# Last modulation row's outer product scaled on VectorE, the other three rows two scalings per piece on ScalarE and stored from its own queue; one more matmul piece ahead of the last norm gradient

## The chip, the cores and the metric

The kernel runs on one core of a Trainium2 chip. The metric is the device time of one execution in microseconds (us), and the number that stands for a kernel is the median of its runs. One further execution is recorded by the hardware profiler; it has a time of its own. Five engines run their own instruction streams in order: TensorE (PE), VectorE (DVE), ScalarE (ACT), GpSimd (POOL) and SyncE (SP). SP, ACT and POOL also issue DMAs from their queues.

## The reference

The kernel computes the forward pass and all gradients of a conditioned block: six modulation rows come from a condition vector, a layer norm is scaled and shifted by them and goes through a spectral mixer (FFT, a learned complex weight, inverse FFT), and a second norm goes through a two-layer MLP.

```python
mod = (silu(c) @ w_mod).reshape(c.shape[0], 6, 1, -1)      # six rows sa, ca, ga, sb, cb, gb of 1024
h = layernorm(x) * (1 + ca) + sa
x = x + ga * irfft2(rfft2(h) * (w_r + 1j * w_i))           # x is 2048 x 1024
h = layernorm(x) * (1 + cb) + sb
x = x + gb * (gelu(layernorm(h) @ w1 + b1) @ w2 + b2)      # w1 is 1024 x 3584
# outputs: x, and the gradients of x, w_r, w_i, w1, b1, w2, b2, c and w_mod (1024 x 6144)
```

Two of the gradients matter here. The gradient of `w1` (1024 x 3584, `out_4`) is a product over 2048 tokens. The gradient of `w_mod` (`out_9`) is an outer product: column block r of it, 1024 x 1024, is `u = silu(c)` times the gradient `gmod[r]` of modulation row r. The same row also goes, multiplied by `w_mod` and summed, into the gradient of `c`.

## The kernel before, in words

The last stretch of the program, some 90 us, is the gradient of `w1`. A generator, `pieces`, cuts it into pieces of matrix products; `fill(n)` writes out the next n of them. A plain piece is one 128 x 512 block: 16 matmuls over the 16 token chunks into a PSUM accumulator `gw1acc` (four of them rotate under one tag), a cast by ACT into a ring of eight `gwo` buffers, and a store by POOL. Feature groups 0 to 4 are done so. Groups 5 and 6 go together (`gw1_quads`) by seven products in place of eight: a piece there is two products of 8 matmuls each, ACT copies an accumulator into `snap`, DVE adds accumulators and snaps into `gwo`, and some accumulators are cast straight into `gwo`. The second product into an accumulator `gqy` may only start when ACT has copied the first out into `snap`. Its operands (`ct`, `gzh`) are sums that DVE makes beforehand in `quad_sums`. The PE writes out its pieces in one fixed order.

Other work is written out between the pieces, and each engine runs its own share in order:

- `consume_bwd(i, ...)` is the last of the backward mixer, called for four chunks of tokens. Chunk 3 makes the last norm gradient. DVE reduces rows into `s1c` (`scaled_rows`) and `sc` (`ln_bwd`), ACT scales (L1368), `fill` puts plain pieces between. At its end the column sum `accCA` is halved (ACT copy, DVE sum into `rows`) and stored to DRAM as `gmod[1]` by two DMAs of SP (L229).
- After it, `gmod[0]` is made: ACT copies `accSA` into `sr`, DVE folds `sr` and casts it to `row` (L200), and SP stores that row (L201).
- `gmod_chain` goes over rows 4, 2, 1, 0 and eight 128 x 1024 blocks of `w_mod` for each: SP loads the row, broadcast to 128 partitions, into `gr` (L1279, one buffer per row) and the blocks into a ring of four `wrw` (L1280, four steps ahead), and DVE multiplies and sums (L1287). Ten of its 32 steps are written ahead of the loop below.
- `gmod_scaled` goes over the same rows and makes `out_9`: 32 scalings of `gr` by a column of `u_rt` into a ring of five buffers `otl`, each then stored (256 KB).

The loop that closes the program takes the last 23 pieces, n = 0 to 22: the first eight are the plain pieces of group 4, the others fifteen of the sixteen quad pieces. Behind each piece it writes out chain steps (from n = 7 on) and scalings: one for n below 14, two from 14 on. The last piece follows the loop, beside the gradient of `c` (`gc_bf`, a product `ptr`).

DMAs issued by SP and by ACT count their landing on eight counters, DMAHW0 to DMAHW7, dealt out in turn in the order of the program. In the rows below, what a DMA "waits" on can therefore be data, or the previous DMA with the same counter, which must have landed first. DMAs of POOL have counters of their own (DMASW).

Of the kernel before, what the change touches and what calls it, by code (L numbers as in the profile page):

```python
# [13 lines left out]
ACT = mybir.ActivationFunctionType  # L14
ALU = mybir.AluOpType
AX = mybir.AxisListType

P = 128
S = 2048
D = 1024  # L20
# [15 lines left out]
def kernel(  # L36
# [24 lines left out]
    nc = tc.nc  # L61
# [11 lines left out]
    def ps_s(name):  # L73
        return psum.tile([P, 512], FP32, tag="s", name=name)
# [51 lines left out]
    def chunk_rows(dt, i):  # L126
        return dt[4 * i * P:4 * (i + 1) * P, :].rearrange("(q p) d -> p q d", p=P)
# [14 lines left out]
    def load_tok(t4, src, i, eng=None):  # L142
        s3 = tok_flat(src)
        ins = (eng or nc.sync).dma_start(out=tok_plain(t4, i), in_=tok_rows(s3, i, 0, D))
        for q in range(2):
            nc.gpsimd.indirect_dma_start(out=t4[:, tok_idx(i, q), :], out_offset=None, in_=s3,
                                         in_offset=bass.IndirectOffsetOnAxis(ap=xidx[:, 2 * i + q:2 * i + q + 1], axis=0))
        return ins
# [45 lines left out]
    def tt(out, a, b, op):  # L194
        return nc.vector.tensor_tensor(out=out, in0=a, in1=b, op=op)  # L195
# [125 lines left out]
    def unfold_d(o4, tmp):  # L321
        n = o4.shape[1]
        ov = o4.rearrange("p c (a b w) -> p c a b w", b=2, w=256)
        tv = tmp.rearrange("p c (s b w) -> p c s b w", s=2, w=256)
        tt(tv[:, :, 0], ov[:, :, :, 0, :], ov[:, :, :, 1, :], ALU.add)
        tt(tv[:, :, 1], ov[:, :, :, 0, :], ov[:, :, :, 1, :], ALU.subtract)
        fwd = o4.rearrange("p c (b w) -> p c b w", w=512)[:, :, :, 0:256]
        rev = bass.AP(tensor=o4.tensor, offset=o4.offset + 1023, ap=[o4.ap[0], [D, n], [-512, 2], [-1, 256]])
        tt(fwd, tv[:, :, :, 0, :], tv[:, :, :, 1, :], ALU.add)
        tt(rev, tv[:, :, :, 0, :], tv[:, :, :, 1, :], ALU.subtract)  # L330

    def unfold_tok(o4, tmp):
        tt(tmp[:, 0:4:2, :], o4[:, 0:4:2, :], o4[:, 1:4:2, :], ALU.add)
        tt(tmp[:, 1:4:2, :], o4[:, 0:4:2, :], o4[:, 1:4:2, :], ALU.subtract)
        tt(o4[:, 0:4:3, :], tmp[:, 0:2, :], tmp[:, 2:4, :], ALU.add)
        tt(o4[:, 1:3, :], tmp[:, 0:2, :], tmp[:, 2:4, :], ALU.subtract)
# [84 lines left out]
    for cl, colv, modn in ((CE, kev, 2048), (SE, kev, 2048), (CO, kod, 4096), (SO, kod, 4096)):  # L421
        rows, n = (rowo, 4) if cl % 2 else (rowe, 2)
# [87 lines left out]
    def norm_act(out4, in4, row, i, qs=range(4)):  # L510
        norm_in[0] = ()
        for q in qs:
            t = 4 * i + q
            norm_in[0] += (nc.scalar.activation(out=out4[:, q, :], in_=in4[:, q, :], func=ACT.Identity,  # L514
                                                scale=stats[:, row, 0, t:t + 1], bias=stats[:, row, 1, t:t + 1]),)
# [17 lines left out]
    def ph_out(fc, j, pp):  # L533
        ph2 = phs[fc % 4]
        q = (0, 2, 3, 1)[j]
        ov = ph2[:, :, q * P:(q + 1) * P]
        pv = pp[:, :].rearrange("p (i w) -> p i w", w=P)
        copy = nc.any.tensor_copy if fc <= PH_EARLY else nc.vector.tensor_copy if fc >= PH_KEEP and j > 1 else nc.scalar.copy
        with tc.high_priority():
            copy(out=ov, in_=pv)  # L540
        if j == 3:
            nc.gpsimd.dma_start(out=d_ph[fc * P:(fc + 1) * P, :], in_=ph2.rearrange("p i w -> p (i w)"))

    def ph_part(fc, js):
        for j in js:
# [3 lines left out]
                                              start=(cch == 0), stop=(cch == NDC - 1))  # L549
            ph_out(fc, j, pp)  # L550

    turn_in = [None, None]

    def turn_go(j, cch):
# [20 lines left out]
    for j in range(4):  # L575
        n = 0
# [33 lines left out]
    def gen_rows():  # L610
# [5 lines left out]
        nc.gpsimd.tensor_scalar(out=em1[:, 1, 4:6, 255:256], in0=em1[:, 0, 4:6, 255:256], scalar1=1.0 / (S * D), scalar2=None, op0=ALU.mult)  # L616
        nc.gpsimd.dma_start(out=d_E[:], in_=em1[:])
        return em1

    def behind(ins, later):  # L620
        tc.add_manual_dep(ins.ins, later.ins.name, mybir.DependencyInfo(mybir.DependencyClass.NoSync, mybir.DependencyReason.DATA),
                          reason="order")

    last_pu = [None]
    last_po = [None]
# [19 lines left out]
    w1g = {}  # L645
# [606 lines left out]
    u_rt = small.tile([P, NDC], FP32, tag="u_rt", bufs=1)  # L1252
# [40 lines left out]
    def gmod_scaled(rows):  # L1293
        for n in range(len(rows) * NDC):
            k, jc = n // NDC, n % NDC
            gw, r = w1g["gw"][n % 5], rows[k]
            with tc.issue_after(w1g["ev"].ins):
                nc.scalar.activation(out=gw, in_=w1g["gr"][k], func=ACT.Identity, scale=u_rt[:, jc:jc + 1])
            nc.gpsimd.dma_start(out=out_9[jc * P:(jc + 1) * P, r * D:(r + 1) * D], in_=gw)
            yield  # L1300

    step_in = []
# [276 lines left out]
    accCA = []  # L1579

    chain, scaled = gmod_chain((4, 2, 1, 0)), gmod_scaled((4, 2, 1, 0))
    prods = []

    def consume_bwd(i, o4, tmp, tmp2, n1, eb):
        if i == 0:
            accCA.append(ps_s("accCA"))
            nc.vector.tensor_copy(out=sacc, in_=eb[:, 0, :])
        elif i == 2:
            tt(sacc, sacc, eb[:, 0, :], ALU.add)
        if i == 3:  # L1590
            x1_in = nc.sync.dma_start(out=eb, in_=chunk_rows(d_gx1, i))
        unfold_d(o4, tmp)
        unfold_tok(o4, tmp)
        load_tok(n1, A_x, i, nc.gpsimd)
        with tc.issue_after(last_po[0].ins):
            norm_act(n1, n1, 0, i)
        prods.append(tt(tmp, o4, n1, ALU.mult))
        fill((0, 6, 6, 8)[i])
        s1c = small.tile([P, 4], FP32, tag="s1c")
        scaled_rows(o4, o4, opca_row, s1c, 0, i)  # L1600
        for q in range(4):
            ln_bwd(o4[:, q, :], s1c[:, q:q + 1], n1[:, q, :], tmp2[:, q, :],
                   (lambda: tc.issue_after(w1g["ev"].ins)) if i else ExitStack)
        if i < 3:
            x1_in = nc.sync.dma_start(out=n1, in_=chunk_rows(d_gx1, i))
        tt(o4, o4, n1 if i < 3 else eb, ALU.add)
        store_tok(out_1, o4, i)
        if i == 1:
            with tc.issue_after(x1_in.ins):
                next(chain)  # L1610
        fill((4, 1, 2, 2)[i])
        halves_sum(accCA[0], tmp, i == 0, i == 3)
        fill((1, 2, 1, 2)[i])
        if i == 3:
            rows = small.tile([P, D], BF16, tag="gmrow", bufs=1)
            store_halves(accCA[0], rows[0:64, 0:KH], tmp, 1)
# [165 lines left out]
    def fill(n):  # L1782
        for _ in range(n):
            next(todo)
        done[0] += n
# [28 lines left out]
    with tc.issue_after(fm_in.ins):  # L1814
        for jc in range(NDC):
            wr = wr5[jc // 4][:, jc % 4, :]
            nc.vector.tensor_tensor_reduce(out=wr, in0=wr, in1=gr5[:], scale=1.0, scalar=0.0,
                                           op0=ALU.mult, op1=ALU.add, accum_out=gu[:, 5, jc:jc + 1])
# [39 lines left out]
    left = NFC * 4 - 1 - done[0]  # L1858
    for n in range(left):
        fill(1)  # L1860
        k = [(32 - CHAIN_EARLY) * min(max(n + 17 + j - left, 0), 14) // 14 for j in range(2)]
        for _ in range(k[1] - k[0]):
            with tc.issue_after(w1g["dve"].ins):
                next(chain)
        for _ in range(2 if n >= left - 9 else 1):
            next(scaled, None)
    fin2 = reg.tile([P, 2, P], BF16, name="fin2", tag="ph")
    make_identity(nc, fin2[:, 0, :])
# [41 lines left out]
```

## Time and profile before

| what | value |
|---|---|
| median of 3 runs | 1373.33 us (1371.58, 1376.87, 1373.33) |
| the profiled execution, its own time | 1372.29 us |
| its span in the profile | 1370.3 us |
| mean granted clock of TensorE | 0.997 |
| ACT scalings `otl<-gr,u_rt` | 32, from 1291.3 us to 1361.3 us |
| last ACT cast into `gwo` begins | 1363.14 us |
| DVE, ACT, POOL busy | 79%, 58%, 28% of the span |

The span is the profiler's, from the first to the last instruction that it records; the execution's time is 2.0 us longer. All positions in time below are counted from the start of the span. In the timeline a row is a start, a length, the engine, the source line, what it does, a count, and in brackets how long the engine sat idle before it and what released it. SPq and ACTq are the issuing of DMAs by those engines.

### The profile page before, as it was taken

What the parts mean: (1) busy time and instruction counts of PE and PEld (TensorE: products, weight loads), DVE (VectorE), ACT (ScalarE), POOL (GpSimd) and SP (SyncE); (2) the same over time, 40 slices, a digit from 0 to 9 for tenths busy, and PEclk for the clock granted to TensorE, in tenths of its full rate; (3) what the DMA queues carried; (4) which work ended last, traced back from release to release, by engine and by line L of the source; (5) the groups of instructions that cost most, each with busy time, mean ns of one, the idle gap of its engine ahead of it and who ended that gap; (6) DMA issues with size and microseconds to landing.
All of it is one profiled execution on the core that took longest, in us unless ns stands there. A gap on an engine that the chain in (4) does not pass through costs nothing. (4 is left out here: it accounts for less than half of the span.)

```text
span 1370.3 us, 18631 instructions
## 1 busy us (share of the span) xinstructions
PE 1345.6 (98%) x6899; PEld 651.0 (48%) x6899; DVE 1077.2 (79%) x1467; ACT 792.4 (58%) x1120; POOL 390.3 (28%) x436
## 2 busy tenths in 40 slices
PE   7999999999999999999999999999999999999997
PEld 4445566444444444444444444444644555444443
DVE  6997889999988878787620578889888488976985
ACT  4864667767877765665414593445732554544456
POOL 6273642411112122212211010112344330332163
PEclk9999999999999999999999999999999999999999
DMA  9975594899787887698999699988579878899876
GB/s 326 322 196 140 160 256 154 250 279 318 262 254 252 212 261 246 199 289 233 284 278 224 181 217 311 296 254 257 179 238 270 222 160 237 207 245 251 201 271 244
DMA packets 356401, 330.08 MB, mean 241 GB/s; under 512 B 203866, under 2 KB 298736, under 8 KB 356182
## 3 DMA queue, kind: packets, MB, share of 16 engines
q1 hardware_dynamic: 314310, 201.02, 57.2%
q0 software_dynamic: 35232, 120.00, 26.0%
q10 hardware_dynamic: 6768, 7.87, 1.7%
q8 instruction: 54, 0.88, 0.3%
q14 instruction: 37, 0.30, 0.1%
HBM read 165.73 MB, written 114.87 MB: 205 GB/s over the span
## 5 line engine op out<-in xcount | busy, mean ns | idle before, releaser
L1230 PE MATMUL pg<-w1T,gzr 128*128 128x512 bf16 x896 | 195.8, 380 | 0.0
L548 PE MATMUL pp<-gBoT,wt 128*128 128x512 bf16 x832 | 185.4, 379 | 3.2 <-ACT pho L540 1.9
L1076 PEld LDWEIGHTS <-w 128*128 128x128 bf16 x896 | 87.2, 98 | 107.4 <-issue 2.9
L1230 PEld LDWEIGHTS <-gzr 128*128 128x128 bf16 x896 | 86.5, 98 | 108.5 <-issue 5.8
L548 PEld LDWEIGHTS <-wt 128*128 128x128 bf16 x832 | 81.0, 98 | 97.9 <-issue 5.3
L1770 PE MATMUL gw1acc<-gzh,n3n 128*128 128x512 bf16 x512 | 111.8, 380 | 0.0
L1076 PE MATMUL pz<-n3Ta,w 128*128 128x512 bf16 x448 | 98.8, 380 | 1.4 <-ACT gt L1079 1.4
L1076 PE MATMUL pz<-n3Tb,w 128*128 128x512 bf16 x448 | 99.0, 380 | 0.0
L1770 PEld LDWEIGHTS <-n3n 128*128 128x128 bf16 x640 | 62.3, 98 | 76.7 <-issue 3.1
L195 DVE TENSOR_TENSOR ct<-ct 128x2048 bf16<-128x2048 bf16 (+1 forms) x84 | 91.5, 1120 | 4.3 <-ACT n L514 2.0
L1079 ACT ACTIVATE gt<-pz,b_col 128x512 bf16<-128x512 f32 x112 | 72.8, 682 | 37.3 <-PE pz L1076 33.1
L1130 PEld LDWEIGHTS <-hhA 128*128 128x128 bf16 x608 | 58.9, 98 | 73.2 <-issue 3.0
L1087 ACT ACTIVATE gt<-gt 128x2048 bf16<-128x2048 bf16 x28 | 53.5, 1911 | 58.3 <-DVE gt L195 58.3
L1411 PE MATMUL gw2acc<-gB,hhsA 128*128 128x512 bf16 x384 | 84.8, 380 | 0.0
L195 DVE TENSOR_TENSOR gt<-gt,gt 128x2048 bf16<-128x2048 bf16 x56 | 68.4, 1223 | 17.7 <-ACT gt L1089 16.8
L1419 ACT CAST gwo<-gw2acc 128x512 bf16<-128x512 f32 x40 | 23.5, 588 | 87.5 <-PE gw2acc L1411 84.2
L1411 PEld LDWEIGHTS <-hhsA 128*128 128x128 bf16 x384 | 37.5, 98 | 43.5
L1083 ACT ACTIVATE gt<-gt 128x2048 bf16<-128x2048 bf16 x28 | 53.4, 1908 | 3.1 <-DVE hhC L195 2.4
L540 ACT CAST pho<-pp 128x512 bf16<-128x512 f32 x68 | 38.6, 584 | 27.3 <-PE pp L548 24.1
L1774 ACT CAST gwo<-gw1acc 128x512 bf16<-128x512 f32 x40 | 23.0, 579 | 53.6 <-PE gw1acc L1770 41.6
L1089 ACT ACTIVATE gt<-gt 128x2048 bf16<-128x2048 bf16 x28 | 53.3, 1905 | 0.3
L1411 PE MATMUL gw2acc<-gB,otl 128*128 128x512 bf16 x224 | 50.0, 380 | 0.0
(414 smaller groups left out, 2710.3 us busy)
## 6 DMA issues: line engine op xcount, KB each, us to landing
gzr<-d_gz SPq DMA_DIRECT2D x28, 512.0 KB
d_ph<-pho POOLq DMA_DIRECT2D x21, 512.0 KB, 5.5
wblk<-in_w_mod_dram SPq DMA_DIRECT2D x10, 1024.0 KB
out_dram<-otl POOLq DMA_DIRECT2D x40, 256.0 KB, 4.1
d_hh<-hhA POOLq DMA_DIRECT2D x19, 512.0 KB, 5.6
wrw<-in_w_mod_dram SPq DMA_DIRECT2D x32, 256.0 KB
w<-in_B_w_dram SPq DMA_DIRECT2D x7, 1024.0 KB
hhC<-d_ph SPq DMA_DIRECT2D x14, 512.0 KB
```

The costliest lines, as they stand in the source:

```text
L195: return nc.vector.tensor_tensor(out=out, in0=a, in1=b, op=op)
L540: copy(out=ov, in_=pv)
L548: last_pe[0] = nc.tensor.matmul(pp[:], lhsT=wt[:, fc % 4, cch, :], rhs=gBoT[j][:, cch, :], start=(cch == 0), stop=(cch == NDC - 1))
L1076: last_pe[0] = nc.tensor.matmul(pz[:], lhsT=w1s[g][:, cch, k * P:(k + 1) * P], rhs=n3T[:, cch, :], start=(cch == 0), stop=(cch == NDC - 1))
L1079: z_in = nc.scalar.activation(out=zb[:, k, :], in_=pz[:], func=ACT.Identity, bias=b1_col[:, fc:fc + 1], scale=1.0)
L1083: nc.scalar.activation(out=av, in_=zb, func=ACT.Square)
L1087: nc.scalar.activation(out=sg, in_=bv, func=ACT.Sigmoid, scale=2.0 * GK)
L1089: nc.scalar.activation(out=bv, in_=bv, func=ACT.Sigmoid, scale=-2.0 * GK)
L1130: last_pe[0] = nc.tensor.matmul(pbs[i][:], lhsT=hh[:, k, i * P:(i + 1) * P], rhs=wp[:, k, :], start=False, stop=(g == 6 and k == 3))
L1230: last_pg[0] = nc.tensor.matmul(pgs[i][:], lhsT=gzs[b, g][:, k, i * P:(i + 1) * P], rhs=w1Ts[g][:, k, h * KH:(h + 1) * KH], start=(g == 0 ...
L1411: nc.tensor.matmul(acc[:], lhsT=hh_of(fc)[:, t, :], rhs=gBs[t // 4][:, t % 4, h * KH:(h + 1) * KH], start=(t == 0), stop=(t == NT - 1))
L1770: nc.tensor.matmul(acc[:], lhsT=n3ns[t // 4][:, t % 4, cch * P:(cch + 1) * P], rhs=gz2[t // 8][:, t % 8, :], start=(t == 0), stop=(t == NT ...
```

## The change

Three parts. In `gmod_scaled`, the scalings of the last row (row 0, k = 3) run on DVE as a `tensor_scalar`, chained behind the DVE work before them, and are stored by POOL as before; those of rows 4, 2 and 1 stay on ACT, and their stores are issued from ACT's own queue. In the loop, the scalings are written out at another pace: two behind each of the pieces n = 0 to 7 (all of rows 4 and 2), one behind each of n = 9 to 16 (row 1), two behind each from n = 18 on until all are written (row 0). In `consume_bwd`, chunk 3 writes nine pieces instead of eight ahead of its `scaled_rows`, and one instead of two later. The function `behind` is only moved up in the file.

```diff
-            with tc.issue_after(w1g["ev"].ins):
-                nc.scalar.activation(out=gw, in_=w1g["gr"][k], func=ACT.Identity, scale=u_rt[:, jc:jc + 1])
-            nc.gpsimd.dma_start(out=out_9[jc * P:(jc + 1) * P, r * D:(r + 1) * D], in_=gw)
+            if k < 3:
+                with tc.issue_after(w1g["ev"].ins):
+                    nc.scalar.activation(out=gw, in_=w1g["gr"][k], func=ACT.Identity, scale=u_rt[:, jc:jc + 1])
+            else:
+                with tc.issue_after(w1g["dve"].ins):
+                    w1g["dve"] = nc.vector.tensor_scalar(out=gw, in0=w1g["gr"][k], scalar1=u_rt[:, jc:jc + 1], scalar2=None,
+                                                         op0=ALU.mult)
+            (nc.scalar if k < 3 else nc.gpsimd).dma_start(out=out_9[jc * P:(jc + 1) * P, r * D:(r + 1) * D], in_=gw)
...
-        fill((0, 6, 6, 8)[i])
+        fill((0, 6, 6, 9)[i])
...
-        fill((4, 1, 2, 2)[i])
+        fill((4, 1, 2, 1)[i])
...
-        for _ in range(2 if n >= left - 9 else 1):
+        for _ in range(2 if n < 8 else 1 if 8 < n < 17 else 2 if n >= left - 5 else 0):
             next(scaled, None)
```

In the changed kernel the line numbers near the end of the file are higher by up to five: the scaling on ACT is L1299, its store L1304, the cast of a plain piece L1779, the snap L1673.

What the change does to the order of instructions is shown at three places. The first is ACT, at the end of the plain pieces and up to the first `snap` of the quads (`gwo<-gw1acc` is the cast of a plain piece, `otl<-gr,u_rt` a scaling). Before:

```order
L1774 CAST gwo_9683<-gw1acc 128x512 [waits DMASW2_49,PE_49,Activation_49]
L1298 ACTIVATE otl<-gr,u_rt 128x1024 [waits DMASW0_49,Activation_49]
L1774 CAST gwo_9683<-gw1acc 128x512 [waits DMASW5_49,PE_49]
L1298 ACTIVATE otl<-gr,u_rt 128x1024 [waits DMASW2_49,Activation_49]
L1774 CAST gwo_9683<-gw1acc 128x512 [waits DMASW6_49,PE_49]
L1298 ACTIVATE otl<-gr,u_rt 128x1024 [waits DMASW4_49,Activation_49]
L1668 COPY snap<-gqy 128x512 [waits DMAHW2_49,DVE_49,PE_49]
```

The same place on ACT after the change; the first row is the ninth of the stores of `otl`:

```order
L1304 DMA out_dram<-otl 128x1024 [waits DMAHW7_49,Activation_49]
L1299 ACTIVATE otl<-gr,u_rt 128x1024 [waits DMAHW2_49]
L1299 ACTIVATE otl<-gr,u_rt 128x1024 [waits DMAHW3_49]
L1304 DMA out_dram<-otl 128x1024 [waits DMAHW0_49,Activation_49]
L1779 CAST gwo_9683<-gw1acc 128x512 [waits DMASW3_49,PE_49]
L1304 DMA out_dram<-otl 128x1024 [waits DMAHW1_49,Activation_49]
L1299 ACTIVATE otl<-gr,u_rt 128x1024 [waits DMAHW5_49]
L1299 ACTIVATE otl<-gr,u_rt 128x1024 [waits DMAHW6_49]
L1779 CAST gwo_9683<-gw1acc 128x512 [waits DMASW6_49,PE_49]
L1304 DMA out_dram<-otl 128x1024 [waits Activation_49] x2
L1673 COPY snap<-gqy 128x512 [waits DVE_49,PE_49]
```

Each cast now has two scalings and the issue of two stores beside it, and every store that shows a DMAHW counter waits for an earlier DMA of SP or ACT to land before ACT goes on.

The second place is SP's queue, where the two `gmod` rows are stored and loaded again. Before:

```order
L165 DMA out_dram<-ct 128x2x1024 [waits DMAHW6_49,DVE_49,Activation_49]
L229 DMA d_gmod<-rows 1x512 [waits DMAHW7_49,DVE_49]
L229 DMA d_gmod<-rows 1x512 [waits DMAHW0_49]
L1279 DMA gr<-d_gmod 128x1024 [waits DMAHW7_49,DMAHW1_49,DMAHW0_49]
L201 DMA d_gmod<-row 1x1024 [waits DMAHW2_49,DVE_49]
L1280 DMA wrw<-in_w_mod_dram 128x1024 [waits DMAHW3_49,DVE_49]
L1280 DMA wrw<-in_w_mod_dram 128x1024 [waits DMAHW4_49,DVE_49]
L1279 DMA gr<-d_gmod 128x1024 [waits DMAHW5_49,DMAHW2_49]
```

The same place after; the first `gr<-d_gmod` is that of row 1, the second that of row 0:

```order
L229 DMA d_gmod<-rows 1x512 [waits DMAHW6_49,DVE_49]
L229 DMA d_gmod<-rows 1x512 [waits DMAHW7_49]
L165 DMA out_dram<-ct 128x2x1024 [waits DMAHW0_49,DVE_49,Activation_49]
L1279 DMA gr<-d_gmod 128x1024 [waits DMAHW7_49,DMAHW6_49,DMAHW1_49]
L201 DMA d_gmod<-row 1x1024 [waits DMAHW4_49,DVE_49]
L1279 DMA gr<-d_gmod 128x1024 [waits DMAHW4_49]
L1280 DMA wrw<-in_w_mod_dram 128x1024 [waits DMAHW0_49,DVE_49]
L1280 DMA wrw<-in_w_mod_dram 128x1024 [waits DMAHW1_49,DVE_49]
```

Before, SP's DMAs take the counters 6, 7, 0, 1, 2, 3, 4, 5 in turn, none left out. After, they take 6, 7, 0, 1, then 4, 7, 0, 1: the ones between went to ACT's stores, the load of `gr` for row 0 has counter 7, and the next counter 7 is that of the ninth `otl` store on ACT. That load now follows directly on the store of the row (L201), ahead of two loads of `wrw`.

The third place is DVE, where `quad_sums` and the row's cast are interleaved. Before:

```order
L195 TENSOR_TENSOR ct<-ct,eb 128x4096
L195 TENSOR_TENSOR rows<-accCA,ct 64x512
L195 TENSOR_TENSOR ct<-ct,n3n_9673 128x2048
L195 TENSOR_TENSOR ct<-n3n_9675,ct 128x2048
L195 TENSOR_TENSOR ct<-n3n_9677,ct 128x2048
L195 TENSOR_TENSOR gzh_9681<-gzh_9679,gzu_10360 128x4096
L195 TENSOR_TENSOR gzh_9682<-gzh_9680,gzh_9681 128x4096
L195 TENSOR_TENSOR sr<-sr 1x512 x2
L195 TENSOR_TENSOR gzh_9679<-gzh_9680,gzh_9679 128x4096
L195 TENSOR_TENSOR sr<-sr 1x2x256 x2
L195 TENSOR_TENSOR ct<-gzu_10361,gzh_9682 128x4096
L200 CAST row<-sr 1x512 x2
```

After:

```order
L195 TENSOR_TENSOR rows<-accCA,ct 64x512
L195 TENSOR_TENSOR ct<-ct,eb 128x4096
L195 TENSOR_TENSOR ct<-ct,n3n_9673 128x2048
L195 TENSOR_TENSOR gzh_9681<-gzh_9679,gzu_10360 128x4096
L195 TENSOR_TENSOR ct<-n3n_9675,ct 128x2048
L195 TENSOR_TENSOR sr<-sr 1x512 x2
L195 TENSOR_TENSOR gzh_9682<-gzh_9680,gzh_9681 128x4096
L195 TENSOR_TENSOR sr<-sr 1x2x256 x2
L195 TENSOR_TENSOR gzh_9679<-gzh_9680,gzh_9679 128x4096
L200 CAST row<-sr 1x512 x2
L195 TENSOR_TENSOR ct<-n3n_9677,ct 128x2048
L195 TENSOR_TENSOR ct<-gzu_10361,gzh_9682 128x4096
```

The cast of the row has moved ahead of two sums, `ct<-n3n_9677,ct` (2048 elements a partition) and `ct<-gzu_10361,gzh_9682` (4096), and the sum `rows` ahead of `ct<-ct,eb`; the rest is the same work in another order.

More of the change, by code (lines that the diff above doesn't have):

```diff
@@ L550, in ph_part, with behind @@
             ph_out(fc, j, pp)
+    def behind(ins, later):
+        tc.add_manual_dep(ins.ins, later.ins.name, mybir.DependencyInfo(mybir.DependencyClass.NoSync, mybir.DependencyReason.DATA),
+                          reason="order")
     turn_in = [None, None]
@@ L618, in gen_rows @@
         return em1
-    def behind(ins, later):
-        tc.add_manual_dep(ins.ins, later.ins.name, mybir.DependencyInfo(mybir.DependencyClass.NoSync, mybir.DependencyReason.DATA),
-                          reason="order")
     last_pu = [None]
```

## The prediction

> **What bounds the kernel now.** The page first: the span and the engines' busy time.
>
> ```profile
> span 1370.3 us, 18631 instructions
> PE 1345.6 (98%) x6899; PEld 651.0 (48%) x6899; DVE 1077.2 (79%) x1467; ACT 792.4 (58%) x1120; POOL 390.3 (28%) x436
> ```
>
> PE is busy all but 24.7 us of 1370.3, so nothing that another engine saves counts unless it closes a gap of PE, and whatever opens one costs its full length. The change lies in the last 90 us; the windows view (PE, PEld, DVE, ACT, POOL busy, clock, DMA share, GB/s) shows where PE is idle there.
>
> ```profile
> 1250.00:1300.00 50.00, 48.49 (x231) 21.64 (x229) 41.55 (x51) 16.87 (x24) 9.66 (x13) 1.00 0.93 216
> 1300.00:1330.00 30.00, 30.00 (x141) 13.57 (x139) 26.80 (x33) 16.07 (x20) 22.38 (x29) 1.00 0.76 259
> 1330.00:1350.00 20.00, 20.00 (x95) 9.04 (x93) 16.39 (x28) 14.47 (x17) 8.96 (x17) 1.00 0.95 334
> ```
>
> From 1300 to 1350 PE has no idle time, ACT is half empty, and DVE is nearly full up to 1330. The only gap is 1.51 us before 1300. The timeline shows it.
>
> ```profile
> 1282.68 3.52 ACT L1368 ACTIVATE ct<-xt,s1c,sc 128x1024 bf16<-128x1024 bf16 x3 [11.70 <-DVE s1c L1359]
> ...
> 1286.72 27.79 PE L1770 MATMUL gw1acc<-gzu,n3n 128*128 128x512 bf16 x128 [1.51 <-ACT gwo L1774]
> ```
>
> ACT stands at the norm's scaling, which waits 11.70 us for DVE, the casts queue behind it, and PE runs out of accumulators. That gap is all that can be won here; the rest of PE's idle time lies outside the change's reach, at the two ends of the span above all.
>
> **The change part by part.** *One more piece ahead of the norm* puts one cast ahead of that wait: PE gets an accumulator more, worth one piece, 27.79/8 = 3.5 us (the row's 128 matmuls are eight pieces), and the gap of 1.51 us closes: **−1.5**, if nothing later waits.
>
> *Two scalings per cast with their stores on ACT.* ACT's scalings, all of them and five in a row:
>
> ```profile
> L1298 ACT ACTIVATE otl<-gr,u_rt x32: 1134/1148/1162, 1291.3 to 1361.3; 128x1024 bf16<-128x1024 bf16 x32
> ...
> 1334.06 5.30 ACT L1298 ACTIVATE otl<-gr,u_rt 128x1024 bf16<-128x1024 bf16 x5
> ```
>
> One of 1.148 us overlaps the next; in a row of five it takes 5.30/5 = 1.06. What a store issued by ACT costs is seen on the earlier stores of the other weight gradient, which went out from ACT's queue (minimum, median and maximum in ns, first and last start), and on one of them with the cast behind it:
>
> ```profile
> L1421 ACTq DMA_DIRECT2D out_dram<-gwo x36: 338/338/398, 997.4 to 1166.4; - x36
> L1421 ACTq EVENT_SEMAPHORE  x31: 17/17/17, 996.7 to 1161.0; - x31
> ...
> 1040.03 0.34 ACTq L1421 DMA_DIRECT2D out_dram<-gwo  x1
> 1040.47 0.79 ACT L906 CAST cs01b<-pcs 128x512 bf16<-128x512 f32 x1
> ```
>
> It keeps ACT for 0.44 us (1040.03 to 1040.47). A piece then costs ACT 2 x 1.06 + 2 x 0.44 + a cast of 0.5 = 3.5 us against PE's 3.5 us: level, so by itself nothing, with four accumulators as slack.
>
> *The stores' waits* are what I price highest. In the order after the change the fourth and the ninth store wait for the DMA that had their counter before. The rows of SP's queue, and what it waited for longest there:
>
> ```profile
> 1299.91 0.72 SPq L229 DMA_DIRECT2D d_gmod<-rows  x2
> 1302.32 0.35 SPq L1279 DMA_DIRECT2D gr<-d_gmod  x1
> 1315.47 0.21 SPq L201 DMA_DIRECT2D d_gmod<-row  x1
> 1316.60 1.50 SPq L1280 DMA_DIRECT2D wrw<-in_w_mod_dram  x2
> 1318.20 1.21 SPq L1279 DMA_DIRECT2D gr<-d_gmod  x1
> 1319.50 10.63 SPq L1280 DMA_DIRECT2D wrw<-in_w_mod_dram  x6
> ...
> SPq L201 <- DVE row L200: 12.7, 1, 12.7
> ...
> SPq L1279 <- DMA d_gmod<-rows: 1.5, 1, 1.5
> ```
>
> The fourth store waits for the landing of the column sum's store (L229). Its issue ended at 1300.63 and the load that needs it went out at 1302.32, so landing takes 1.7 to 2.4 us. These rows of DVE say when the two stored rows are ready:
>
> ```profile
> 1297.00 2.29 DVE L195 TENSOR_TENSOR ct<-ct,eb 128x4096 bf16<-128x4096 bf16 x1
> ...
> 1300.94 2.34 DVE L195 TENSOR_TENSOR ct<-n3n,ct 128x2048 bf16<-128x2048 bf16 x2
> ...
> 1312.40 2.27 DVE L195 TENSOR_TENSOR ct<-gzu,gzh 128x4096 bf16<-128x4096 bf16 x1
> 1314.60 0.84 DVE L200 CAST row<-sr 1x512 bf16<-1x512 f32 x2
> ```
>
> After the change the sum `rows` comes ahead of `ct<-ct,eb` (2.3 us), so L229 lands near 1300 instead of 1302.3. ACT gets to the fourth store two pieces after its first scaling at about 1291, near 1298, and is held some 2 us; the casts behind it have four accumulators of 3.5 us each as cover: costed at nothing (without the cover, 2).
>
> The ninth store waits for the load of `gr` for row 0, the last link of a chain: the fold of `sr`, the cast of the row on DVE, its store, its load. Before, nothing on ACT hung on it until the last eight scalings. The cast ended at 1315.44 and moves ahead of half of the first row (1.17) and all of the second (2.27): 1315.44 − 3.44 = **1312.0**. From the row's store to its load issued I take the 2.3 us above (1299.91 to 1302.32 is 2.4): **1314.3**. SP has nothing else in between now. The load's landing has no row of its own; loads of the same 256 KB do, by the DVE step that waits for them:
>
> ```profile
> 1288.33 3.77 SPq L1280 DMA_DIRECT2D wrw<-in_w_mod_dram  x4
> ...
> 1292.07 1.23 DVE L1287 CUSTOM_DVE_ANT_0 wrw<-wrw,gr 128x1024 bf16<-128x1024 bf16 x1 [0.33 <-DMA wrw<-in_w_mod_dram]
> ...
> 1321.54 1.23 DVE L1287 CUSTOM_DVE_ANT_0 wrw<-wrw,gr 128x1024 bf16<-128x1024 bf16 x1 [0.93 <-DMA wrw<-in_w_mod_dram]
> ...
> 1326.80 1.23 DVE L1287 CUSTOM_DVE_ANT_0 wrw<-wrw,gr 128x1024 bf16<-128x1024 bf16 x1 [1.33 <-DMA wrw<-in_w_mod_dram]
> ```
>
> At 1288.33 it took 3.7 us to the step at 1292.07; the load of 1316.60 took 4.9 (to 1321.54), that of 1319.50 took 7.3 (to 1326.80). Those late ones shared the DMA engines with stores that POOL sent one upon the other:
>
> ```profile
> 1308.75 1.67 POOL L1775 DMA_DIRECT2D out_dram<-gwo  x3
> ...
> 1317.85 0.54 POOL L1299 DMA_DIRECT2D out_dram<-otl  x1
> ```
>
> Between these rows lie 18 stores in 9.6 us, eight of them of `otl`; after the change those go out from ACT, spread over time, and none while ACT is held. So I take 3.7, with 2.1 (about the small store's) and 7.3 as ends. `gr` lands at **1318.0**.
>
> ACT reaches the ninth store near 1308: the first scaling at about 1291, four pieces of 3.5, the hold of 2 us above and one scaling. It then stands until 1318.0, with two casts and the first `snap` of the quads behind it. PE waits for that `snap`:
>
> ```profile
> 1317.15 0.58 ACT L1668 COPY snap<-gqy 128x512 f32<-128x512 f32 x1
> ...
> 1317.80 1.89 PE L1686 MATMUL gqy<-gzh,ct 128*128 128x512 bf16 x8
> ```
>
> What ACT does from 1318.0, by the order after: a store 0.44, two scalings 2.12, a store 0.44, a cast 0.5, a store 0.44, two scalings 2.12, a cast 0.5, two stores 0.88, the `snap` 0.58: 8.0 us. (The tenth and eleventh store wait for the two `wrw` loads; issued some 2 us after `gr` and a step apart, they land as ACT gets there.) PE goes on at 1326.0 in place of 1317.80: **+8.2**. The −1.5 is not added: PE would only come to the wait earlier, and what ends the wait is DVE's chain.
>
> *Row 0 on DVE*, eight scalings:
>
> ```profile
> L1322 DVE TENSOR_SCALAR otl<-otl,u_rt x8: 476/482/486, 1009.4 to 1071.7; 128x1024 bf16<-128x1024 bf16 x8
> ...
> 1353.79 0.17 DVE L1876 CAST gc_bf<-t 128x8 bf16<-128x8 f32 x1
> 1354.31 0.69 DVE L195 TENSOR_TENSOR gwo<-gqx,snap 128x512 bf16<-128x512 f32 x1 [0.36 <-PE gqx L1686]
> ...
> 1359.33 0.22 PE L210 MATMUL ptr<-fin,gc_bf 128*8 128x128 bf16 x1
> ```
>
> Seven of 0.48 and the sum of 0.69, which comes ahead now, move the end of `gc_bf` from 1353.96 to 1358.1, still 1.2 us ahead of the product `ptr`; both slide together with PE. Costed at nothing; without that cover, 1 to 2 us. POOL loses 24 store issues that nobody on PE's path waits for. The end is not touched: the last cast of a quad and its store follow PE's last piece as now.
>
> The sum, against the profiled execution's own time: 1372.29 + 8.2 = 1380.5. The median of the runs stood 1.0 us above that execution, so **1381.5**. With a landing of 2.1 us it is 1.6 less, 1379.9; with 7.3 it is 3.6 more, 1385.1.
>
> **The rivals.** *The stores wait for nothing.* The 31 semaphore waits of ACT's stores L1421 took 17 ns each: on that queue a store's wait has so far been free. Then only the gap's closing is left: 1373.33 − 1.5 = 1371.8. It decides at the ninth store: `gr` would have to land by 1308 and not at 1318.0. Against it: SP's queue waited 12.7 us for that row, and L1421 ran where SP's loads were long landed. [...] *The late loads stay slow*, 7.3 us as before: 1385.1. *The hold is covered and DVE's last scalings delay `ptr`* by 1 to 2 us: with −1.5 about 1373.3.
>
> **How the numbers follow.** Hold with a landing of 2.1 to 4.9 us: 0.60. Slow loads: 0.17. No hold: 0.18. Late `ptr` alone: 0.05. Within 0.5% (1366.5 to 1380.2, about what a measurement of this kernel can tell from no change) lie both covered cases save 0.04 that are faster still, and a fifth of the main one: 0.18 + 0.05 − 0.04 + 0.12 = 0.31. Faster 0.04, slower 0.48 + 0.17 = 0.65. The range takes in the ends of the unknown landing with the spread of the runs (1.8 below, 3.5 above the median) and part of the covered cases: 1374 to 1387.
>
> **What would show it.** A PE gap of some 9 to 10 us that ends near 1326 at `gqy<-gzh,ct`, released by ACT's `snap`; a semaphore wait of L1304 on ACT of about 9 to 10 us that ends when `gr` lands; one of about 2 us five stores earlier; no gap of PE at 1286; the row's cast near 1312. Wrong would be: all L1304 waits at 17 ns, or a long wait with PE still busy (then ACT's slack was larger than I count), or a PE gap at `ptr`.

## The result, and the profile after

| | before | after |
|---|---|---|
| median of the runs (10 of each) | 1374.03 us (1370.77 to 1382.58) | 1384.24 us (1377.55 to 1388.84) |
| ratio, after to before | | 1.0067, 95% interval 1.0047 to 1.0086 |
| the profiled execution, its own time | 1372.29 us | 1388.84 us |
| its span | 1370.3 us | 1387.0 us |

The changed kernel is slower by 0.67% of 1374, 9.2 us; the medians stand 10.2 us apart. Its profiled execution is the slowest of its ten, so its span is taken apart before anything is read from it. First the page and the windows view of the kernel after (PE, PEld, DVE, ACT, POOL busy, clock, DMA share, GB/s).

```profile
span 1387.0 us, 18600 instructions
...
PE 1347.2 (97%) x6899; PEld 651.8 (47%) x6899; DVE 1082.2 (78%) x1475; ACT 785.9 (57%) x1112; POOL 386.5 (28%) x412
...
1250.00:1300.00 50.00, 48.34 (x231) 21.68 (x230) 34.88 (x44) 19.18 (x26) 10.35 (x14) 1.00 1.04 235
1300.00:1330.00 30.00, 23.25 (x108) 10.45 (x107) 25.37 (x27) 12.89 (x15) 17.18 (x9) 0.94 0.55 190
1330.00:1350.00 20.00, 13.74 (x55) 5.81 (x55) 9.44 (x17) 13.12 (x16) 3.10 (x6) 0.75 0.80 255
```

PE, which had no idle time from 1300 to 1350, lost 13.0 us of it there, and its granted clock fell to 0.75 in the window behind. The timeline of PE:

```profile
1284.11 0.62 PE L218 MATMUL accCA<-ct,ones_bf 128*32 128x512 bf16 x8 [1.66 <-DVE ct L195]
...
1292.01 27.79 PE L1775 MATMUL gw1acc<-gzu,n3n 128*128 128x512 bf16 x128
...
1336.26 3.57 PE L1691 MATMUL gqy<-gzh,ct 128*128 128x512 bf16 x8 [13.01 <-ACT snap L1673]
1339.63 2.16 PE L1691 MATMUL gqw<-gzh,ct 128*128 128x512 bf16 x8
```

The plain pieces of group 4 start at 1292.01 where they started at 1286.72, 5.3 us later. Of that, 5.2 us are there earlier, ahead of everything that the change touches (the column sum of the chunk before stands at 1236.77 and at 1241.99). They are mostly the luck of this execution: in e1 and e10 below, the same program up to there, that sum stands at 1237.56 and 1238.22. Their old gap of 1.51 us is gone, and one of 1.66 us stands before the column sum instead. Then comes the new gap, 13.01 us (13.2 from start to start), at the place that the prediction named, and the two groups of eight products behind it take 5.4 us in place of 3.5: 1.9 us of low clock. These make 20.4 us. The span grew by only 16.7, so 3.7 us were won at the end. The instructions of the closing line, by name, before:

```profile
L1905 POOLq DRAIN  x3: 51/103/6763, 1362.7 to 1370.0; - x3
```

and after:

```profile
L1910 POOLq DRAIN  x3: 51/103/5632, 1378.6 to 1386.7; - x3
```

The three numbers are the minimum, the median and the maximum in ns; a drain is an instruction of that closing line. Before, it began at 1362.7 behind the last store of `otl`, took 6.76 us to 1369.5, and the semaphore instructions of this line on PE, ACT and DVE, two each, all start behind it, at 1369.7 or later; from the end of the last cast (1363.72) to the end of the span passed 6.6 us. After, POOL's last store goes out 5 us before the last cast, the drain is over at 1384.2, and the same stretch (from 1384.11) takes 2.9 us. Net, for the change itself: 13.2 + 1.9 + 0.1 − 3.7 = +11.5 us in this execution, beside 9.2 in the comparison of all.

What filled the gap is in ACT's timeline after:

```profile
1306.61 0.34 ACTq L1304 DMA_DIRECT2D out_dram<-otl  x1
1306.99 2.19 ACT L1299 ACTIVATE otl<-gr,u_rt 128x1024 bf16<-128x1024 bf16 x2 [1.46 <-DMA d_gmod<-rows]
...
1324.14 0.34 ACTq L1304 DMA_DIRECT2D out_dram<-otl  x1
1324.53 2.19 ACT L1299 ACTIVATE otl<-gr,u_rt 128x1024 bf16<-128x1024 bf16 x2 [10.70 <-DMA gr<-d_gmod]
1331.23 0.34 ACTq L1304 DMA_DIRECT2D out_dram<-otl  x1
1331.66 0.59 ACT L1779 CAST gwo<-gw1acc 128x512 bf16<-128x512 f32 x1 [4.95 <-DMA wrw<-in_w_mod_dram]
...
1335.62 0.59 ACT L1673 COPY snap<-gqy 128x512 f32<-128x512 f32 x1
```

A bracket here names the work after the wait, though the store ahead of it did the waiting. The fourth store was held 1.46 us by the column sum's store, the ninth 10.70 us by the load of `gr`. Then comes a third wait that the prediction counted as none: 4.95 us for a load of `wrw`. Those loads are freed by steps on DVE (SP waited up to 7.2 us for one of them between 1300 and 1345), and DVE and SP show why they were late:

```profile
1318.39 0.74 DVE L200 CAST row<-sr 1x512 bf16<-1x512 f32 x2
1319.07 1.21 DVE L195 TENSOR_TENSOR ct<-n3n,ct 128x2048 bf16<-128x2048 bf16 x1
1324.87 2.29 DVE L195 TENSOR_TENSOR ct<-gzu,gzh 128x4096 bf16<-128x4096 bf16 x1 [4.59 <-issue]
...
1319.16 0.23 SPq L201 DMA_DIRECT2D d_gmod<-row  x1
1320.74 0.33 SPq L1279 DMA_DIRECT2D gr<-d_gmod  x1
1328.33 12.39 SPq L1280 DMA_DIRECT2D wrw<-in_w_mod_dram  x6
```

The sum `ct<-gzu,gzh` overwrites rows of `ct` that POOL still stores as the last chunk of `out_1`. "issue" in the bracket means that the profile shows no releaser; in the program the sum has to wait for POOL's two indirect stores, and e10 below shows that it did. Their rows, before:

```profile
1299.58 6.81 POOL L167 DMA_INDIRECT out_dram<-ct,xu  x1 [10.46 <-DVE ct L195]
1306.69 2.06 POOL L167 DMA_INDIRECT out_dram<-ct,xu  x1 [0.30 <-issue]
```

and after:

```profile
1307.47 11.90 POOL L167 DMA_INDIRECT out_dram<-ct,xu  x1 [10.01 <-DVE ct L195]
1319.67 1.48 POOL L167 DMA_INDIRECT out_dram<-ct,xu  x1 [0.30 <-issue]
```

The first of the two takes 11.90 us instead of 6.81. The next `wrw` loads thus went out at 1328.33, 7.6 us behind the load of `gr` (1320.74); I had expected some 2 us.

### The profile page after: what moved, and what is told of

Same layout as the page of the kernel before. It is cut to its first block, busy times and chain, and to the rows that moved or that the text cites. A ratio compares the mean times of both kernels' runs of the same rounds, so it can differ in the third digit from the quotient of the medians.

```text
span 1387.0 us, 18600 instructions
## 1 busy us (share of the span) xinstructions
PE 1347.2 (97%) x6899; PEld 651.8 (47%) x6899; DVE 1082.2 (78%) x1475; ACT 785.9 (57%) x1112; POOL 386.5 (28%) x412
## 5 line engine op out<-in xcount | busy, mean ns | idle before, releaser
L1779 ACT CAST gwo<-gw1acc 128x512 bf16<-128x512 f32 x40 | 22.9, 579 | 54.7 <-PE gw1acc L1775 43.4
```

## The experiments

The theory after the result (A): ACT is held because its stores share completion counters with SP's loads, most of all the ninth with the load of `gr` for row 0; POOL's longer indirect store adds a second hold through DVE; the last row on DVE is a gain. Rivals: two scalings per cast are too much for ACT (B), only the counters cost anything (C), or the extra piece is what loses. All medians below stand beside runs of the kernel before on the same chip, and ratios are to those.

**e1: all stores back on POOL.** In the changed kernel:

```diff
-            (nc.scalar if k < 3 else nc.gpsimd).dma_start(out=out_9[...], in_=gw)
+            nc.gpsimd.dma_start(out=out_9[...], in_=gw)
```

> All stores of the scalings issued by POOL again; the pace of two scalings per piece, the extra piece and the last row on VectorE stay. Theory A (ACT's stores wait for the DMA that had their completion counter): no wait on a counter is left on ACT, but the ring of five buffers is filled faster than before, and POOL stands in the two indirect stores of the last norm gradient (6.8 to 11.9 us for the first in the two profiles), so the sixth scaling waits for POOL: a PE gap of 6 to 15 us again, the same size as with ACT's queue, now released through DMA out_dram<-otl. Rival B (two scalings per cast are simply too much work for ACT): a gap of about the same size with ACT busy and not waiting. Rival C (only the counters cost anything): no PE gap, some 1368 to 1371 us.

Measured: 1386.68 us against 1373.66, ratio 1.0090 (1.0064 to 1.0116). ACT and PE of this run:

```profile
1320.59 1.15 ACT L1299 ACTIVATE otl<-gr,u_rt 128x1024 bf16<-128x1024 bf16 x1 [20.91 <-DMA out_dram<-otl]
...
1322.26 6.48 PE L1775 MATMUL gw1acc<-gzu,n3n 128*128 128x512 bf16 x16 [10.92 <-ACT gwo L1779]
```

Rival C falls. Taking the counters away alone is no cure at this pace: the sixth scaling wants a buffer whose store stands behind POOL's indirect store, which took 11.90 us here too, and ACT waits 20.91 us. ACT's own queue avoids that wait, at the price of the counters. B gets no support here: ACT waited and did not work.

**e2: only the first eight stores on ACT's queue**, in the changed kernel:

```diff
-            (nc.scalar if k < 3 else nc.gpsimd).dma_start(out=out_9[...], in_=gw)
+            (nc.scalar if k < 1 else nc.gpsimd).dma_start(out=out_9[...], in_=gw)
```

> Only the first eight stores (row 4) go out from ACT's queue, the others from POOL; all else as in the changed kernel. Theory A: the ninth store no longer waits for the load of gr for row 0, the long PE gap ahead of gqy<-gzh,ct shrinks from 13 us to 0 to 4 us (work that ACT has still to catch up), and the time is 1370 to 1374 us, since the shorter end of the changed kernel (POOL drained before the last cast) stays. Rival B (ACT overloaded by two scalings per piece): the gap stays at 8 us or more and the time at 1380 or more. Either way the fourth store is held some 2 us by the landing of the column sum, with no PE gap.

Measured: 1375.04 us against 1373.66, ratio 1.0017 (0.9997 to 1.0037).

```profile
1316.00 1.15 ACT L1299 ACTIVATE otl<-gr,u_rt 128x1024 bf16<-128x1024 bf16 x1 [3.44 <-DMA out_dram<-otl]
...
1320.23 1.89 PE L1691 MATMUL gqy<-gzh,ct 128*128 128x512 bf16 x8 [2.57 <-ACT snap L1673]
```

The gap is 2.57 us in place of 13.01, with the same pace, the same extra piece and the same work on ACT; the profile is of one of the shorter of its runs (1370.85 us), but the interval of the ratio, too, lies wholly below that of the change. So the counter waits from the ninth store on were the larger part of the loss, as A has it, and B falls. The time is 1 us above the range forecast; its twelve runs spread from 1369.9 to 1383.0, which the runs of the extra piece alone, below, explain in part.

**e3: the last row on VectorE alone**, in the kernel before (the pace, the fill and POOL's stores as they were):

```diff
+            if k < 3:
                 with tc.issue_after(w1g["ev"].ins):
                     nc.scalar.activation(out=gw, in_=w1g["gr"][k], func=ACT.Identity, scale=u_rt[:, jc:jc + 1])
+            else:
+                with tc.issue_after(w1g["dve"].ins):
+                    w1g["dve"] = nc.vector.tensor_scalar(out=gw, in0=w1g["gr"][k], scalar1=u_rt[:, jc:jc + 1], scalar2=None, op0=ALU.mult)
```

> The kernel before with one part of the change: the scalings of the last row on VectorE, stored by POOL. Theory A: the end gets shorter, because POOL has its last store out before the last cast: the drain of POOL, which ended 5.8 us after the last cast in the profile before, ends with it, worth 3 to 4 us; the PE gap of 1.5 us stays. About 1370.5 against 1374. Rival: the end is set by the last landing of the weight gradient anyway and the scalings delay the product ptr: 1373 to 1376.

Measured: 1369.76 us against 1373.66, ratio 0.9977 (0.9962 to 0.9993): this part alone is a gain. POOL and ACT at the end of its profile, whose span is 1367.5 us:

```profile
1359.39 1.08 POOL L1304 DMA_DIRECT2D out_dram<-otl  x2 [2.73 <-DVE otl L1302]
...
1361.65 0.58 ACT L1681 CAST gwo<-gqy 128x512 bf16<-128x512 f32 x1 [4.81 <-PE gqy L1691]
```

POOL's last store still goes out only 1.7 us before the last cast, so its drain still ends last: 5.3 us pass from the last cast's end to the end of the span, 6.6 before. So the drain gives 1.3 us, less than expected. The profile's span is 2.8 us shorter than before, and the other 1.5 us are the gap ahead of the plain pieces of group 4: it is absent in this execution (they start at 1285.22, against 1286.72), though the pieces are written out as before. Whether the medians, 3.2 us apart by the ratio with an interval down to 1.0, owe part to that isn't shown.

**e4: ACT's queue alone**, at the old pace, fill and last row:

```diff
-            nc.gpsimd.dma_start(out=out_9[...], in_=gw)
+            (nc.scalar if k < 3 else nc.gpsimd).dma_start(out=out_9[...], in_=gw)
```

> The kernel before with one part of the change: the stores of rows 4, 2 and 1 issued from ACT's queue, at the old pace, the last row on ACT and stored by POOL. Theory A: ACT is held by the counters here too, at a scaling or store whose counter belongs to the store or load of the row (7 to 9 us of waiting near 1317), with fewer scalings to catch up: a PE gap of 4 to 8 us ahead of gqy<-gzh,ct, the end as before, 1377 to 1382. Rival B (only the doubled pace costs): no gap beside the 1.5 us of before, 1373 to 1375.

Measured: 1380.32 us against 1373.66, ratio 1.0044 (1.0027 to 1.0062).

```profile
1316.81 0.58 ACT L1774 CAST gwo<-gw1acc 128x512 bf16<-128x512 f32 x1 [7.79 <-DMA d_gmod<-row]
...
1323.13 3.30 PE L1686 MATMUL gqy<-gzh,ct 128*128 128x512 bf16 x8 [5.42 <-ACT snap L1668]
```

The queue by itself loses about 6 us, with one scaling per piece, no extra piece and nothing moved to DVE. At this pace the counter belongs to the row's store (L201), not its load. POOL's first indirect store took 6.81 us.

**e5: the extra piece alone**, in the kernel before, **and e11**, the same once more for a second profile:

```diff
-        fill((0, 6, 6, 8)[i])
+        fill((0, 6, 6, 9)[i])
...
-        fill((4, 1, 2, 2)[i])
+        fill((4, 1, 2, 1)[i])
```

> The kernel before with one part of the change: nine pieces ahead of the last norm gradient. Theory A: the gap of 1.5 us at the norm closes, but the order on VectorE that comes with it keeps POOL's indirect store 11.9 us instead of 6.8, so that the sum ct<-gzu,gzh on VectorE waits 4 to 5 us for that store and the ring of otl waits longer for POOL (gap of 0 to 5 us ahead of gqy<-gzh,ct): 1372 to 1378, no gain. Rival (what I forecast for this part): the gap closes and nothing else waits, 1372.5 or less, with POOL's store at 6.8 us.

> The extra piece alone once more, for a profile of another execution: five of seven runs took 1377 to 1380 us, and the profile at hand (1370.8 us, no PE gap) shows a fast one. Theory A (POOL, kept 11.9 us by VectorE, has its stores late, and ACT's sixth scaling waits for a buffer): in a slow execution POOL's second indirect store takes several us instead of 1.5, ACT waits 9 us or more for the buffer instead of 5.2, and PE has a gap of 4 to 7 us ahead of a quad. Rival: a slow execution loses its time elsewhere in the program, with no gap in the last 90 us.

Measured: 1377.62 us against 1372.96, ratio 1.0033 (1.0013 to 1.0053), its seven runs from 1370.83 to 1379.97; the first profile is of the fastest, the second of an execution of 1380.22 us. POOL and ACT of the first:

```profile
1293.02 11.90 POOL L167 DMA_INDIRECT out_dram<-ct,xu  x1 [9.91 <-DVE ct L195]
...
1311.60 1.15 ACT L1298 ACTIVATE otl<-gr,u_rt 128x1024 bf16<-128x1024 bf16 x1 [5.15 <-DMA out_dram<-otl]
```

and POOL, ACT and PE of the second:

```profile
1300.52 11.89 POOL L167 DMA_INDIRECT out_dram<-ct,xu  x1 [9.96 <-DVE ct L195]
...
1319.15 1.15 ACT L1298 ACTIVATE otl<-gr,u_rt 128x1024 bf16<-128x1024 bf16 x1 [10.99 <-DMA out_dram<-otl]
...
1323.87 3.57 PE L1686 MATMUL gqy<-gzh,ct 128*128 128x512 bf16 x8 [5.97 <-ACT snap L1668]
```

The extra piece is a loss by itself, and the second execution lost its time where A has it: its span is 9.4 us longer, and the gap of 5.97 us, 1.8 us of low clock behind it and the 1.7 us of a later start make that up. In both the buffer comes free 18.6 us after POOL begins its first indirect store, but that store began 7.5 us later in the second, while PE's plain pieces of group 4 began 1.7 us later (1284.95 and 1286.65). What I expected of the second store (several us) did not happen; it took 1.48 in both. So the norm's chain on DVE runs early or late against PE from one execution to the next, here by some 6 us; over all fourteen profiles that store begins 8.0 to 15.5 us behind the plain pieces of group 4, and 15.5 is the changed kernel's. With POOL's store at 11.9 us in both, the late one of these two has the PE gap of 5.97 us, and the early one has none.

**e7: the changed kernel without the extra piece** (the fill of 8 and 2 as before, all else as changed).

> The changed kernel with the old eight pieces ahead of the norm gradient; stores, pace and last row as changed. Theory A: POOL's indirect store is back at 6.8 us and the sum ct<-gzu,gzh no longer waits, but the row is cast later, and ACT is held by the counter of the row's store (L201) at an earlier store than the ninth, some 10 to 12 us: a PE gap of 10 to 14 us in one or two parts, 1380 to 1386. Rival (the extra piece makes the loss): the gap is gone or under 3 us, 1372 or less.

Measured: 1379.18 us against 1372.96, ratio 1.0063 (1.0039 to 1.0088).

```profile
1315.36 2.19 ACT L1299 ACTIVATE otl<-gr,u_rt 128x1024 bf16<-128x1024 bf16 x2 [11.70 <-DMA d_gmod<-row]
...
1318.07 1.44 PE L1691 MATMUL gqy<-gzu,n3n 128*128 128x512 bf16 x3 [5.07 <-ACT gwo L1779]
...
1326.75 3.30 PE L1691 MATMUL gqy<-gzh,ct 128*128 128x512 bf16 x8 [2.74 <-ACT snap L1673]
```

The loss is as large as the whole change's (1.0067), so the extra piece isn't needed for it. The hold of 11.70 us, at the sixth store, is in the range expected, POOL's store is at 6.82 us, and DVE's long sum has no wait. The two gaps add to 7.8 us, less than the 10 to 14 forecast, and some 3.7 us of low clock stand behind them; the time is 0.8 us under its range.

On their own, ACT's queue (+0.44%), the extra piece (+0.33%) and the last row on DVE (−0.23%) make +0.54%, and the whole change has +0.67%. The new pace alone, with nothing else changed, was not run.

**e10: the sum `ct<-gzu,gzh` in a tile of its own**, in the changed kernel:

```diff
-        S1, S2, S4, T4 = (rows8(w1g["ct"][:, k]) for k in range(4))
+        S1, S2, S4 = (rows8(w1g["ct"][:, k]) for k in range(3))
+        T4 = reg.tile([P, 8, KH], BF16, name="T4", tag="px0")[:]
```

> The changed kernel with the sum ct<-gzu,gzh written to a tile of its own (the one of sr, free after the row's cast), so that it no longer waits for POOL's stores of ct. Theory A (the second half of the hold comes from that wait, through the steps on VectorE that free wrw and the loads behind them): VectorE loses its 4.6 us wait, the wrw loads go out 4 to 5 us earlier, ACT's second hold of 5 us shrinks to under 1.5, the PE gap from 13 to 8 to 10 us, about 1380. Rival (that wait lies beside the gr load's hold and costs nothing): gap 12 to 13 us, 1384.

Measured: 1378.13 us, ratio 1.0041 (1.0026 to 1.0056), against 1.0067 (1.0047 to 1.0086) for the change.

```profile
1316.97 2.19 ACT L1299 ACTIVATE otl<-gr,u_rt 128x1024 bf16<-128x1024 bf16 x2 [8.96 <-DMA gr<-d_gmod]
1320.12 0.58 ACT L1780 CAST gwo<-gw1acc 128x512 bf16<-128x512 f32 x1 [0.96 <-DMA wrw<-in_w_mod_dram]
...
1322.24 2.19 ACT L1299 ACTIVATE otl<-gr,u_rt 128x1024 bf16<-128x1024 bf16 x2 [1.53 <-DMA wrw<-in_w_mod_dram]
...
1325.72 3.57 PE L1692 MATMUL gqy<-gzh,ct 128*128 128x512 bf16 x8 [7.96 <-ACT snap L1674]
```

The hold by `gr` stays. DVE's sum follows the one before it without a wait, and the two holds by `wrw` fall from 4.95 and 0.72 us to 0.96 and 1.53. So the second hold came through DVE's wait for POOL, as A has it. The gap falls from 13.01 to 7.96, but only 3.0 of these 5.1 us lie behind the ninth store, where the edit acts; the other 2.1 lie ahead of it, because the row's chain ran earlier against PE in this execution. The intervals of the two ratios overlap, so the time saved isn't measured apart.

**Versions meant to keep the gains alone.** From the kernel before with the last row on DVE and all other stores on POOL: nine pieces and a slow pace (e9), the same with a more even pace behind the quads (e12), and e12 with the last row's stores issued by SP (e14); and with eight pieces and the old pace, the last row's stores issued by SP (e13).

The pace, in the order e9, then e12 and e14, and the store in e13 and e14:

```diff
-        for _ in range(2 if n >= left - 9 else 1):
+        for _ in range(1 if n < 5 else 0 if n < 8 else 2):
```

```diff
-        for _ in range(2 if n >= left - 9 else 1):
+        for _ in range(1 if n < 5 or n in (11, 14, 17) else 0 if n < 8 else 2):
```

```diff
-            nc.gpsimd.dma_start(out=out_9[...], in_=gw)
+            (nc.gpsimd if k < 3 else nc.sync).dma_start(out=out_9[...], in_=gw)
```

> A version meant to keep the gains alone: nine pieces ahead of the norm, last row on VectorE, all stores on POOL, and a pace that never meets a full ring while POOL is in its indirect stores: one scaling behind each of the first five pieces, none behind the next three, two behind each later one. Theory A: no counter wait and no full ring, no PE gap in the last 90 us, the short end: 1367 to 1369.5. Rival: POOL's longer indirect store and its backlog still hold ACT or VectorE near 1312 to 1320: 1371 or more.

> As e9 (nine pieces, last row on VectorE, stores on POOL, nothing behind three pieces while POOL is in its indirect stores), with the scalings on ACT spread more evenly behind the quads: two behind each piece but one behind n = 11, 14 and 17. Theory A: ACT no longer meets a full ring ahead of a snap, the 2.35 us gap of e9's profile at 1333 goes: 1367 to 1369.5, 1 to 2 us under e9. Rival: the gap came from a chance backlog of the stores and the median stays at 1370.

> As e3 (only the last row on VectorE), with the eight stores of that row issued by SP instead of POOL. Theory A (the end of the program waits for POOL, whose drain ends 6.7 us after its last store): POOL's last store goes out some 6 us before the last cast, the end follows SP's last landing, 2.0 to 2.5 us earlier than e3: 1367 to 1368. Rival (the end is set by the landings themselves): as e3, 1369.5.

> e12 with the last row's stores issued by SP. Theory A: no PE gap in the last 90 us and the short end: 1365.5 to 1368.5, the fastest of all. Rival: the end is already set by SP in e12 (its POOL is done early enough), and nothing is gained over it.

| | median | ratio to before |
|---|---|---|
| e9, nine pieces, slow pace | 1370.19 us | 0.9983 (0.9974 to 0.9993) |
| e12, even pace | 1373.66 us | 1.0005 (0.9993 to 1.0017) |
| e13, eight pieces, last row stored by SP | 1368.52 us | 0.9969 (0.9955 to 0.9983) |
| e14, e12 with SP | 1372.92 us | 0.9992 (0.9976 to 1.0007) |

Only e13 came out near its forecast, 0.5 us above its range, and it has the lowest median of the study, 4.2 us under the kernel before. The last cast in its profile, whose span is 1367.7 us:

```profile
1364.24 0.58 ACT L1681 CAST gwo<-gqy 128x512 bf16<-128x512 f32 x1 [4.81 <-PE gqy L1691]
```

From its end to the end of the span pass 2.9 us, as in the kernel after, where e3 has 5.3. Against e3 (0.9977) the intervals overlap, so SP's share isn't measured apart. The three with nine pieces missed their forecasts, e9 by 0.7 us. e9 has a gap of 2.35 us at a quad, by a full ring. In e12 POOL's store began late again, at 1299.67, 13.8 us behind the plain pieces of group 4 (10.4 in e9), and ACT waited 6.59 us for a buffer of the other ring:

```profile
1317.50 0.59 ACT L1779 CAST gwo<-gw1acc 128x512 bf16<-128x512 f32 x1 [6.59 <-DMA out_dram<-gwo]
```

The casts' stores stand behind the same indirect store, so sparing `otl` does not free ACT. And e12 has the long end again, because its pace writes out the last row later: POOL's last store goes out 1.7 us before the last cast.

```profile
1363.34 1.08 POOL L1304 DMA_DIRECT2D out_dram<-otl  x2 [2.76 <-DVE otl L1302]
...
1365.62 0.58 ACT L1681 CAST gwo<-gqy 128x512 bf16<-128x512 f32 x1 [4.81 <-PE gqy L1691]
```

From that cast's end to the end of the span of 1371.4 us pass 5.2 us, and 2.9 in e9: 2.3 of the 4.8 us between the two profiles. Another 1.8 stand there at the start of the plain pieces already. e14 has the short end (2.9 us) and, where no gap was forecast, three that add to 2.8 us. Why its median lies only 0.7 us under e12's isn't settled: one profile of each doesn't tell the pace from the luck of the norm's chain.

## Why the prediction was right, and where its steps were off

- **What bounds it**, PE with ACT's `snap` as the place to lose: right, 13.01 us at `gqy<-gzh,ct`.
- **The ninth store waits for the load of `gr`**: right, shown by the row of 10.70 us, by e2 (the coupling gone, 2.57 us left) and by e4 (the queue alone, ratio 1.0044). The chain's pieces: the row's cast moved 3.7 us ahead within DVE's work (from 22.2 to 18.5 us behind the first sums `ct<-ct`, at 1293.22 and 1300.64), where I took 3.44. It still ended at 1319.13 and not at 1312.0, because PE's plain pieces came 5.3 us later in this execution and DVE's chain another 2.1 behind them. From the row's cast to its load issued were 1.6 us where I took 2.3; the load landed 3.4 us after its issue, near the 3.7 that I took.
- **From that landing to the end of the `snap`, 8.0 us**: this term was mis-sized; it measured 12.1 (1324.14 to 1336.21). I had the tenth and eleventh stores' `wrw` loads land "as ACT gets there". They waited for DVE, and DVE for POOL's indirect store, 5.1 us longer than before. e10 takes that wait away, and the same stretch measures 9.1 us there (1316.59 to 1325.66).
- **The fourth store, about 2 us and covered**: right, 1.46 us and no gap.
- **The closing of the first gap, −1.5 and swallowed**: the gap went, but 1.66 us came back at the column sum. It was no steady gap to win either: of the five profiles with eight pieces ahead of the norm it is 1.51 us in the one I read, 0.53 in e7, and at most 0.1 in e3, e4 and e13. As a part of its own it is no gain but a loss of 0.33% (e5): I had not asked what the new order on DVE does to POOL.
- **Row 0 on DVE, nothing**: the product `ptr` was not delayed, but the end was said to be untouched, and it was 3.7 us shorter. I had read the end as the last cast and its store; it was POOL's drain.
- **The clock**: 1.9 us behind the gap were not in the sum.
- **Slips without weight**: ACT, which I called half empty from 1300 to 1350, was busy for 30.5 of the 50 us; the 2.3 us from the row's store to its load are 2.4 by the rows beside it; and the end of `gc_bf` comes to 1358.0, not 1358.1.

The sum of 8.2 us (9.7 for the hold, less 1.5) stands beside 9.2 by the ratio, and beside 11.5 in the profiled execution. That it came so near is in part luck, because misses were opposite: 3.5 us more hold, 1.6 for the gap that wasn't won, 1.9 of low clock, and −3.7 at the end. The rival "the stores wait for nothing" rested on 31 semaphore waits of 17 ns. That was no evidence: in the kernel after the same instruction shows 17 ns too,

```profile
L1304 ACTq EVENT_SEMAPHORE  x17: 17/17/17, 1300.6 to 1360.8; - x17
```

although one of the seventeen stood before a wait of 10.70 us. On these stores the wait shows as the idle time before the next work, not as the length of that instruction.

## What to carry to other kernels

When a store is moved to another queue, look up which earlier DMA had its completion counter: here an output that shared a counter with an input waited 10.70 us for it, and everything on ACT behind it did too. Ask of every reordering on VectorE what GpSimd's DMAs do meanwhile (POOL's first indirect store took 6.81 us before and 11.90 after), and who waits for those. And read the end of the program from the last instructions of all engines: in the kernel before, what finished last was POOL's drain, 6.76 us of a queue with nothing left to compute. Before a gap of 1.5 us is priced as a gain, look whether a second execution has it.

## What the runs showed of the hardware

POOL's first indirect store of the last chunk took 6.81 or 6.82 us in the five profiles with the old order on DVE (before, e3, e4, e7, e13) and 11.89 or 11.90 in the nine with the new one, whatever else differed. It began in a run of DVE sums (two inputs each) that follow each other without a pause. In all five of the old order it ended 0.90 us after the first pause in that run, of 0.09 us (before: 1305.49, end 1306.39), and in all nine of the new 0.97 or 0.98 us after the cast of the row began (after: 1318.39, end 1319.37). In e10, where the sum behind it no longer waits, the second store is long too, 7.11 us in place of 1.48, and ends 0.9 us after DVE's run stops at 1318.62:

```profile
1312.39 7.11 POOL L167 DMA_INDIRECT out_dram<-ct,xu  x1 [0.31 <-issue]
```

No run here changes DVE's order alone, so that it is this order that holds POOL's store is my reading of these rows and not shown apart. Nor is it shown what lets the store end: before, the second store (1306.69 to 1308.75) ended while such sums went on without a pause, 0.96 us after those on `sr` began at 1307.79, and the first store of the new order outlasted two pairs of the same sums.

POOL's drain began with its last store and took 6.76 us before, 6.80 in e3 and e12, and 5.63 in the kernel after. Before, that store went out 0.4 us before the last cast, and the span ended 6.6 us behind the cast's end; after, it went out 4.9 us before it, and the span ended 2.9 us behind.

After 13.0 us without work PE's next eight products took 3.57 us (the granted clock was 0.64 from 1338 to 1341, and 1.00 from 1341.6 on), and so after 5.97 us (e11) and 7.96 us (e10); after 2.57 us (e2) and 2.35 us (e9) they took 1.89, as without a gap. In e7 a gap of 2.74 us soon behind one of 5.07 was followed by 3.30 us, and in e1 one of 2.86 us by 3.49, at a granted clock of 0.51; ahead of that gap PE had worked 3.6 us at the full clock:

```profile
1335.06 3.49 PE L1691 MATMUL gqy<-gzh,ct 128*128 128x512 bf16 x8 [2.86 <-ACT snap L1673]
```

So in these runs the products behind a gap of 2.86 us were about as slow as those behind one of 13.0 (3.49 and 3.57 us).
